# Splitting the store of one weight gradient: 128 rows from GpSimd become 5 and 55 rows from GpSimd and 68 from SyncE

## The chip, the cores and the metric

The kernel runs on one core of a Trainium2 chip. The metric is the device time of one execution in microseconds (us). Each engine of the core (TensorE or PE, VectorE or DVE, ScalarE or ACT, GpSimd or POOL, SyncE or SP) works through its own list of instructions and waits on semaphores for the others. Data moves between the device memory (DRAM) and the on-chip memory (SBUF, 128 partitions or rows) by 16 DMA engines; SyncE, ScalarE and GpSimd issue such transfers.

## The reference

The forward pass is a residual sum of a cached attention step and a gated MLP, for one token. The output is the forward value and all gradients for a given grad_out.

```python
x = A_x                                   # (1, 1, 640)
xn = _layernorm(x)
# attention: q = xn @ wq, 32 heads of 128; caches k, v are (1, 32, 8192, 128)
#   p = softmax(q k^T / sqrt(128));  o = p v;  A = o @ wo
# MLP: h = silu(xn @ w1) * (xn @ w3);  B = h @ w2
return x + A + B
...
_out, _vjp = jax.vjp(_f, A_x, A_k_cache, A_v_cache, A_wq, A_wo, B_w1, B_w3, B_w2)
_grads = _vjp(grad_out)
```

Each of the 32 heads has a K and a V cache of 8192 x 128 bf16 values, 2 MB each, and a gradient of the same size for both. The gradient of wo (4096 x 640), which the change is about, is an outer product: row (head, d) is o[head, d] times grad_out.

## The kernel before

The program works through the heads one after another. A head's K and V tiles are loaded into slots of the SBUF (10 slots of 128 x 8192 bf16), TensorE transposes and multiplies them (scores, probabilities, output, gradient of the probabilities), and then VectorE overwrites the same slots with the gradients of V and K (`outer`, line 464), which are stored from there. `store` (line 477) issues the 2 MB store and then calls `load_next` (line 122), which loads the next K or V tile into the oldest free slot; that load waits until the store from the slot has landed. All these transfers go through `fifo` (line 104), which issues them from SyncE in program order. The order on every engine is the one in which the program is written; nothing is rescheduled.

The projection weights wq and wo belong to 8 groups of 4 heads. `load_group` (line 109) loads one group's `wq_g` (128 x 5 x 512 bf16) and `wo_g` (128 x 4 x 640 bf16), 640 KB each. After the 4 heads of group g are done, during the next group's heads, the group is finished: in its first head `fin_od`, `fin_pe` and `fin_wo` (called at line 690, 714 and 702), and in the next two heads `fin_wq` in five pieces. `fin_wo` (line 512) overwrites the four 640-wide rows of `wo_g` by g_bc times o on VectorE (line 515) and stores the tile; the last piece of `fin_wq` stores `wq_g` and loads group g+3 into the same buffers (three sets of buffers).

The store itself is in `store_group` (line 505). For groups 0 to 6 it is one transfer of 128 rows from GpSimd (line 507). For group 7, the last, it is two transfers from SyncE: rows 0 to 59 and rows 60 to 127 (lines 509 and 510). In the DRAM a wo row of the tile is four pieces of 1,280 bytes, one for each head; in the SBUF it is one piece of 5,120 bytes.

The MLP is computed between heads 1 and 2 (line 551); its gradients leave from GpSimd. At the very end VectorE and ScalarE form the two small outputs (lines 836 to 862), which ScalarE stores.

`head` (line 740) sets the order around the change: with hh the head's number in its group, for hh = 0 the call of `fin_wo` (in `side_v`, line 782) comes after the K store of the head before and the load behind it (`outers_b`, line 776), and before the V store of the same head, which follows in the next call of `head`.

Of the kernel before, what the change touches and what calls it, by code (L numbers as in the profile page):

```python
# [16 lines left out]
P = 128  # L17
# [4 lines left out]
def kernel(  # L22
# [22 lines left out]
    nc = tc.nc  # L45
# [8 lines left out]
    GH = 4  # L54
# [26 lines left out]
    dwo_v = out_5.rearrange("(h p) c -> p h c", p=P)  # L81
# [22 lines left out]
    def fifo(out_, in_):  # L104
        nc.sync.dma_start(out_, in_)
# [396 lines left out]
        for hh in range(GH):  # L502
            out_row(G_["od_bf"][:, hh, 0:1], G_["wo"][:, hh, :])

    def store_group(g, dst, t):
        if g < NG - 1:
            nc.gpsimd.dma_start(dst, t[:])
            return
        for lo, hi in ((0, 60), (60, P)):
            fifo(dst[lo:hi], t[lo:hi])  # L510

    def fin_wo(g):
        G_ = grp[g]
        for hh in range(GH):
            nc.vector.tensor_scalar(G_["wo"][:, hh, :], g_bc[:], G_["od"][:, hh, 0:1], None, ALU.mult)
        store_group(g, dwo_v[:, g * GH:(g + 1) * GH, :], G_["wo"])

    def fin_wq(g, ci):
        G_ = grp[g]
        wq_g, dqb = G_["wq"], G_["dqb"]  # L520
        nc.vector.scalar_tensor_tensor(wq_g[:, ci, :], wq_g[:, ci, :], 1.0, dqb, ALU.mult, ALU.mult,  # L521
                                       accum_out=dxa[:, ci, g:g + 1])
        nc.vector.tensor_scalar(wq_g[:, ci, :], dqb, xn_col[:, ci:ci + 1], None, ALU.mult)
        if ci == NC - 1:
            store_group(g, dwq_v[:, :, g * GW:(g + 1) * GW], wq_g)
            grp.pop(g)
            if g + 3 < NG:
                load_group(g + 3, nc.gpsimd)
# [170 lines left out]
    def side_v(h):  # L699
        g, hh = divmod(h, GH)  # L700
        if hh == 0 and g > 0:
            fin_wo(g - 1)
        elif hh == 1 and g > 0:
            fin_wq(g - 1, 2)
        elif hh == 2 and g + 1 < NG:
            prep_new(g + 1)
            prep_do(g + 1, 0)
        elif hh == 3 and g + 1 < NG:
            prep_cm(g + 1, hd[h]["m"][:, 324:324 + 4 * GH])
# [120 lines left out]
    fin_od(NG - 1)  # L830
    fin_pe(NG - 1)
    fin_wo(NG - 1)
    for ci in range(NC):
        fin_wq(NG - 1, ci)
# [58 lines left out]
```

## Time and profile before

| | us |
|---|---|
| median of 3 timed runs | 730.84 |
| lowest and highest of them | 729.69, 731.25 |
| profiled execution: span, first to last instruction | 729.3 |
| DMA share of q1 (issued by SyncE and ScalarE) / q0 (issued by GpSimd) | 90.1% / 8.4% |
| data moved, read + written | 151.34 + 151.34 MB |
| mean rate over the span | 416 GB/s |

No other time of the profiled execution is given than its span. The median of the timed runs is 1.5 us above it; differences are worked out within the profile and then added to the median.

A profile page is read like this. "busy" is the time in which an engine executes; the waits say for whom an engine stood idle, and a wait for a DMA names the transfer that landed last. In rows over 40 slices a digit is the busy share in tenths. "DMA" is the mean busy share of the 16 DMA engines: a share of 0.25 is four engines busy. In tables by stretches the columns are the stretch, its length, the busy us of PE, the weight loads (PEld), DVE, ACT and POOL with their instruction counts, then the granted TensorE clock, the DMA share and the rate in GB/s. Entries with SPq are SyncE's transfers and waits. A transfer is cut into packets, each carried by one DMA engine, and each engine reports when its part is done; the trace holds a record of every packet and every such report.

### The profile page before, as it was taken

The page shows a single profiled execution, that of the slowest core. Times are in us where ns is not written, and L with a number is a line of the kernel's source. Part 1 is how long each engine was busy: PE and PEld are TensorE (multiplying, and loading weights), DVE is VectorE, ACT ScalarE, POOL GpSimd, SP SyncE. Part 2 cuts the span into 40 slices and gives each one's busy share as a digit, 9 for nine tenths or more (in the row PEclk, how much of TensorE's full clock was granted, in tenths as well). Part 3 has the DMA queues.
Part 4 walks back from the last instruction along what each step waited for, and adds up shares of the span by engine and source line. Part 5 has one row for each costly group of instructions (what it writes and reads, how often), then busy time and mean ns, then how long its engine had stood idle before and what let it go on. Part 6 is the DMA issues. An engine that isn't in the chain of part 4 may idle for free.

```text
span 729.3 us, 12905 instructions
## 1 busy us (share of the span) xinstructions
PE 600.8 (82%) x5186; PEld 375.4 (51%) x5193; DVE 461.3 (63%) x811; ACT 375.8 (52%) x727; POOL 28.2 (4%) x43
## 2 busy tenths in 40 slices
PE   4989589999999989887897798877897878977930
PEld 2556366665566556554454454544564545544520
DVE  4179646677868886676466755655746765667482
ACT  3740736665666566554465554554564555645510
POOL 0010100000100000001000000000000000000000
PEclk9996799999999999999999999998999999999965
DMA  8999999999999999999999999999999999999994
GB/s 353 404 411 422 427 427 428 417 426 426 414 417 426 430 426 426 428 428 428 422 428 430 428 425 428 427 428 429 424 429 425 430 429 430 428 427 430 430 396 161
DMA packets 28005, 303.53 MB, mean 416 GB/s; under 512 B 2804, under 2 KB 5304, under 8 KB 11304
## 3 DMA queue, kind: packets, MB, share of 16 engines
q1 hardware_dynamic: 22518, 277.70, 90.1%
q0 software_dynamic: 5408, 24.99, 8.4%
q8 instruction: 41, 0.67, 0.4%
q14 instruction: 20, 0.16, 0.1%
q10 hardware_dynamic: 18, 0.01, 0.0%
HBM read 151.34 MB, written 151.34 MB: 415 GB/s over the span
## 4 chain that ended last, share of the span: by engine, by line
DMA 55%; PE 34%; DVE 6%; ACT 2%; issue 1%; SPq 0%; ACTq 0%; DVEq 0%
DMA kv<-in_A_v_cache_dram 21%; DMA out_dram<-kv 18%; PE pT L318 16%; DMA kv<-in_A_k_cache_dram 14%; PE sA L339 5%; PE dA L339 3%; PE X L433 3%; DVE kv L466 3%; PE m L356 2%; DMA wo_g<-in_A_wo_dram 2%; PE gu_ps L556 1%; ACT KT L320 1%; PE dh_ps L567 1%; DVE wq_g L521 1%; PE acc L199 1%
## 5 line engine op out<-in xcount | busy, mean ns | idle before, releaser
L320 ACT COPY KT<-pT 128x512 f32<-128x512 f32 x512 | 287.9, 587 | 230.0 <-PE pT L318 210.3
L318 PE MATMUL pT<-ident_f,kv 128*128 128x128 f32 x2048 | 306.0, 288 | 62.5 <-DMA kv<-in_A_k_cache_dram 35.3
L318 PEld LDWEIGHTS pT<-ident_f,kv 128*128 128x128 f32 x2048 | 235.4, 148 | 155.1 <-PE pT L318 50.0
L466 DVE TENSOR_TENSOR kv<-qd,U 128x4096 bf16<-128x4096 bf16 x64 | 146.1, 2285 | 0.0
L466 DVE TENSOR_TENSOR kv<-qd,P 128x4096 bf16<-128x4096 bf16 x64 | 143.6, 2285 | 0.0
L433 PE MATMUL X<-kv,Z 128*32 128x512 bf16 x1024 | 95.2, 407 | 1.8 <-DVE Z L450 1.8
L339 PE MATMUL dA<-KT,qz 128*32 128x512 bf16 x512 | 83.5, 405 | 0.0
L339 PE MATMUL sA<-KT,qz 128*32 128x512 bf16 x512 | 83.5, 406 | 0.0
L416 DVE SCALAR_TENSOR_TENSOR U<-m,P 128x64 bf16<-128x64 f32 x32 | 7.5, 234 | 87.2 <-PE m L356 87.2
L382 DVE TENSOR_REDUCE mrow<-m 128x1 f32<-128x64 f32 x32 | 7.2, 224 | 69.6 <-PE m L356 69.5
L433 PEld LDWEIGHTS <-Z 128*32 128x32 bf16 x1024 | 33.0, 100 | 34.5 <-issue 7.1
L339 PEld LDWEIGHTS <-qz 128*32 128x32 bf16 x1024 | 29.6, 95 | 40.5 <-issue 38.0
L356 PE MATMUL m<-selc,KT 64*128 64x64 f32 x256 | 30.5, 242 | 7.9 <-ACT KT L346 7.8
L356 PEld LDWEIGHTS m<-selc,KT 64*128 64x128 f32 x256 | 21.5, 144 | 29.9 <-ACT KT L346 20.0
L376 ACT CAST qd<-pT 128x256 bf16<-128x256 f32 x32 | 11.9, 372 | 40.3 <-DVE kv L466 31.6
L389 DVE TENSOR_REDUCE negM<-m 128x1 f32<-128x128 f32 x32 | 9.3, 292 | 33.0 <-PE m L386 33.0
L521 DVE SCALAR_TENSOR_TENSOR wq_g<-wq_g,side 128x512 bf16<-128x512 bf16 x40 | 27.3, 683 | 0.0
L257 DVE SCALAR_TENSOR_TENSOR side<-wo_g,g_bc 128x640 bf16<-128x640 bf16 x32 | 26.2, 820 | 0.7 <-DMA wo_g<-in_A_wo_dram 0.3
L448 DVE SCALAR_TENSOR_TENSOR U<-m,P 128x128 bf16<-128x128 f32 x32 | 11.4, 355 | 16.4 <-PE m L446 16.4
L406 DVE RECIPROCAL rZ<-m 128x1 f32<-128x1 f32 x32 | 5.3, 167 | 24.1 <-PE m L400 24.1
L346 ACT COPY KT<-dA 64x512 f32<-64x512 f32 x32 | 18.6, 582 | 2.9 <-PE dA L339 2.9
L346 ACT COPY KT<-sA 64x512 f32<-64x512 f32 x32 | 18.5, 579 | 2.0 <-PE sA L339 1.7
(161 smaller groups left out, 372.2 us busy)
## 6 DMA issues: line engine op xcount, KB each, us to landing
out_dram<-kv SPq DMA_DIRECT2D x64, 2048.0 KB, 31.0
kv<-in_A_k_cache_dram SPq DMA_DIRECT2D x32, 2048.0 KB, 26.3
kv<-in_A_v_cache_dram SPq DMA_DIRECT2D x32, 2048.0 KB, 26.3
wq_g<-in_A_wq_dram POOLq DMA_DIRECT2D x7, 640.0 KB, 13.4
wo_g<-in_A_wo_dram POOLq DMA_DIRECT2D x7, 640.0 KB, 19.1
out_dram<-wo_g POOLq DMA_DIRECT2D x7, 640.0 KB, 11.9
out_dram<-wq_g POOLq DMA_DIRECT2D x7, 640.0 KB, 13.4
kv<-in_B_w_dram SPq DMA_DIRECT2D x2, 1728.0 KB, 29.2
```

What stands on the lines that cost most here:

```text
L257: nc.vector.scalar_tensor_tensor(junk[:], G_["wo"][:, hh, :], 1.0, g_bc[:], ALU.mult, ALU.mult, accum_out=G_["do"][:, hh:hh + 1])
L318: nc.tensor.transpose(pT[:, k * P:(k + 1) * P], W3[:, 4 * c + k, :], ident_f[:])
L320: nc.scalar.copy(KT[:].rearrange("p k w -> p (k w)"), pT[:])
L339: nc.tensor.matmul(S_[kind][q:q + QW, :], lhsT=S_["qz"][:, o:o + QW], rhs=KTb[c][:, par, :], start=(c0 == 0 and par == 0), stop=(c0 == NCH ...
L346: nc.scalar.copy(XS[0:QH].rearrange("p k w -> p (k w)"), S_.pop(kind)[0:QH, :])
L356: nc.tensor.matmul(S_["m"][:, b0:b0 + 4 * J].rearrange("p (x c k t) -> p k x c t", x=4, k=4, t=2)[:, k], lhsT=XS[0:QH, k, :], rhs=selc[0:Q ...
L376: nc.scalar.copy(qd[:].rearrange("p a d -> p (a d)"), hd[h].pop("ps_r"))
L389: nc.vector.tensor_reduce(S_["negM"][:], S_["m"][:, 2 * J:2 * J + P], AX.X, ALU.max, negate=True)
L433: nc.tensor.matmul(xg["X"][q:q + QW, :], lhsT=Z[:, o:o + QW], rhs=W[:, N4 * i:N4 * (i + 1)], start=(slot == 0 and i < 4), stop=(slot == NS ...
L448: nc.vector.scalar_tensor_tensor(S_["U2"][:], S_["V"][:, 0:J].unsqueeze(2).to_broadcast([P, J, 2]), S_["m"][:, OC + NS:OC + NS + 1], S_["P ...
L466: nc.vector.tensor_tensor(dst[:, lo * DH:hi * DH].rearrange("p (j a b) -> p j a b", a=DH // 2, b=2), vec.rearrange("p (a b) -> p a b", b=2 ...
L521: nc.vector.scalar_tensor_tensor(wq_g[:, ci, :], wq_g[:, ci, :], 1.0, dqb, ALU.mult, ALU.mult, accum_out=dxa[:, ci, g:g + 1])
```

## The change

The store of wo's gradient for groups 1 to 5 leaves as three transfers: rows 0 to 4 and rows 5 to 59 from GpSimd, and rows 60 to 127 from SyncE. Groups 0, 6 and 7 and all of wq's stores stay as they were. Values and bytes are the same.

```diff
-    def store_group(g, dst, t):
+    def store_group(g, dst, t, split=False):
+        if split:
+            for lo, hi in ((0, 5), (5, 60)):
+                nc.gpsimd.dma_start(dst[lo:hi], t[lo:hi])
+            fifo(dst[60:P], t[60:P])
+            return
         if g < NG - 1:
             nc.gpsimd.dma_start(dst, t[:])
             return
...
-        store_group(g, dwo_v[:, g * GH:(g + 1) * GH, :], G_["wo"])
+        store_group(g, dwo_v[:, g * GH:(g + 1) * GH, :], G_["wo"], 1 <= g <= 5)
```

In the instruction lists GpSimd gets five more transfers and SyncE five more; each of SyncE's stands between a load of a K or V tile and the store of the next gradient. The other engines' instructions and their order are the same.

## Prediction

> **What bounds the kernel now.** First I read the page: how busy the engines are and, beside it, what the DMA engines do.
>
> ```profile
> PE 600.8 (82%) x5186; PEld 375.4 (51%) x5193; DVE 461.3 (63%) x811; ACT 375.8 (52%) x727; POOL 28.2 (4%) x43
> DMA  8999999999999999999999999999999999999994
> GB/s 353 404 411 422 427 427 428 417 426 426 414 417 426 430 426 426 428 428 428 422 428 430 428 425 428 427 428 429 424 429 425 430 429 430 428 427 430 430 396 161
> q1 hardware_dynamic: 22518, 277.70, 90.1%
> q0 software_dynamic: 5408, 24.99, 8.4%
> ```
>
> No compute engine is full, but all 16 DMA engines are, from the first slice to the last but one. At 428 GB/s each moves 428/16 = 26.8 GB/s. q1 is what SyncE and ScalarE issue, q0 what GpSimd issues. Next, SyncE's waits:
>
> ```profile
> SPq L105 <- DMA out_dram<-kv: 490.1, 54, 15.1
> SPq L105 <- DVE kv L466: 87.0, 12, 13.4
> ```
>
> SyncE waits 490 us for stores to land before it may load into their buffers; for DVE it waits a fifth of that. So the time is the work of the DMA engines, and what counts is which of the 16 ends last. That is seen in the table by stretches, cut fine at the end (the last two columns are the DMA share and GB/s):
>
> ```profile
> 100.00:690.00 590.00, 516.73 (x4425) 319.59 (x4431) 380.29 (x623) 329.20 (x656) 19.59 (x24) 0.96 1.01 426
> ...
> 718.00:720.00 2.00, 0.00 (x0) 0.00 (x0) 0.00 (x0) 0.00 (x0) 0.00 (x0) 0.50 0.61 197
> 720.00:722.00 2.00, 0.00 (x0) 0.00 (x0) 0.00 (x0) 0.00 (x0) 0.00 (x0) 0.50 0.22 77
> 722.00:725.00 3.00, 0.00 (x0) 0.00 (x0) 0.00 (x0) 0.00 (x0) 0.00 (x0) 0.50 0.32 111
> 725.00:726.00 1.00, 0.00 (x0) 0.00 (x0) 0.00 (x0) 0.00 (x0) 0.00 (x0) 0.50 0.27 94
> 726.00:727.60 1.60, 0.00 (x0) 0.00 (x0) 0.00 (x0) 0.00 (x0) 0.00 (x0) 0.50 0.07 26
> ```
>
> Up to 690 the share is full (1.01). From 722 to 725 it is 0.32, which is five of 16 engines, and after 726 it is 0.07, one engine. The SyncE timeline says what they carry:
>
> ```profile
> 711.74 3.42 SPq L105 DMA_DIRECT2D out_dram<-wo_g  x2
> 715.27 5.96 SPq L105 DMA_DIRECT2D out_dram<-wq_g  x2
> ```
>
> The second issue of the last line, at 720.97, is the 68-row wq store of group 7. In the trace's packet records four engines carry it: 85 packets of 1,024 bytes each, 46 ns apart, from 721.8 to 725.7–726.2. The fifth busy engine is a straggler that is only then finishing its kv stores; it ends at 727.6, 1.7 us before the span does.
>
> The same records give each store's completion engine by engine. The 2 MB store issued at 673.87 was done on five engines by 688.7–689.4, on two at 693.6, on eight at 695.5–699.1, and on the straggler at 706.7. The five keep this lead from about 220 us on; the lag of the others grows slowly. Nobody idles before 690, so an engine that gets more bytes falls behind, and one that gets fewer catches up.
>
> **The change, part by part.** Five times (groups 1 to 5) one 640 KB store from GpSimd becomes three. The bytes stay; their spread over the 16 engines does not.
>
> *The 128-row store that goes.* 128/16 = 8 rows of 5,120 bytes for each engine. Such a packet on q0 takes 200 ns: 8 x 0.20 = 1.6 us off every engine, per group.
>
> *The 68-row store on SyncE.* The nearest row is the same shape in group 7: four engines, 17 rows each. Its 1,280-byte packets run 52 ns apart when undisturbed: 17 x 4 x 52 ns = 3.5 us. Beside other small packets at the end they took 4.0 to 4.5 us. I take 3.5, as the neighbours in mid-run are 16 KB packets, and keep 4.5 for the range.
>
> *The 5- and 55-row stores on GpSimd.* No row shows them. In this trace 60 rows ran on 15 engines, 68 on 4 and 128 on 16, so I expect 5 rows on five engines (one each) and 55 on eleven (five each). Which ones is open: each of the four loaded engines gets 1 row if the two transfers share out the 16, up to 6 if both take the same engines. I take 3, near the mean of 60/16 = 3.75: 0.6 us; ends 0.2 and 1.2.
>
> *Sum.* A loaded engine gains 3.5 + 0.6 - 1.6 = 2.5 us per group, 12.5 us over five (ends: 2.1 x 5 = 10.5 and 4.1 x 5 = 20.5). The others lose 2 to 7 rows per group, 0.4 to 1.4 us; with 5 rows left it is 0.6, 3 us over five. The straggler carried 20, not 105, of the wq packets at the end, so it isn't one of the four: it ends near 724.6.
>
> The Trainium skill ("DMA: Bandwidth & Descriptors", section "Why a DMA increments its semaphore by 16 and not by 1") says that a transfer runs on the largest number of engines up to 16 that divides its rows; 60, 68 and 128 here agree. It adds that on this path fewer than 16 are taken in turn, which no run here shows; by it 5 + 11 share out the 16, the four get 1 row, and the end would come 2 us earlier than I say. The same page's "Rules for kernel authors" speaks against the change: two transfers to disjoint partition ranges gain nothing, since both spread over all 16 engines. The trace differs in one point, as 68 rows did not spread (0.32 of the engines); by the rule as written the time would not move.
>
> *Where the four stand.* In mid-run every transfer runs on all 16 engines, so nothing there tells which four these are; I use the end. A small ScalarE store of one 640-byte packet found its engine idle at 714.5, and one of the four fetched instructions at 715.3 with nothing before it. Seven engines were idle then: the five leaders and the two behind them. I take the four for leaders. They finished the store issued at 684.79 by 694.2. Three kv stores remain, 8 packets of 16 KB at 0.608 us each: 3 x 4.87 = 14.6, so without starving they would be done at 708.8. With 12.5 us more: 721.3. Then group 7: 4 + 17 rows of wo (0.8 + 3.5) and 4 + 17 rows of wq (0.9 + 3.9) = 9.1: 730.4. The end was 727.6, so +2.8 us: a span of 732.1 for 729.3. The median of the runs shown, 730.84, lies 1.5 above that span; the forecast is 730.84 + 2.8 = **733.6 us**.
>
> What they had spare is used in this sum: 4.3 us without work near 696, and about 3 us waiting for the issues at 714.89 and 720.97. It is gone afterwards; late next are the four engines themselves, through the last 68-row store.
>
> *Issues and waits.* Five more issues on GpSimd (0.76 us each) and five on SyncE (0.27 to 0.45) lie in idle time: GpSimd is 4% busy and waits 35 us before such a store. Uncovered they would cost 5 x 1.2 = 6 us of issue time. The new SyncE store waits for DVE's wo_g rows; in program order it stands between a kv load and a kv store. DVE was done at 293.1 in group 2, and SyncE issued that load at 296.31 after a DMA wait, so it finds its data ready. The kv store behind it goes 0.4 us later; the leaders' queue still held 3.1 us when the load at 659.69 was issued. The completion counters of q1 are eight in turn; some kv stores now also wait for the eighth transfer before them. Four load-store pairs of 10.1 us are 40 us, and the slowest landing took 38.4: done, with 2 us to spare. GpSimd's next wo load now waits also for the SyncE part, which lands some 31 to 35 us after 296, before the wq store whose landing released that load's neighbour at 341.43. I count these at nothing.
>
> **The rivals.**
>
> *Faster: the straggler decides.* It sets 727.6 and loses 3 us (5 rows left) or 7 us (1 row left). If the four net under 1.5 us per group, 7.5 in all, their spare time swallows it and they end at 726 or a little earlier, since the last issues come after loads that no longer wait as long. For it: the straggler's 18 us lag. Against: 17 rows for 8 can't well net under 2.1. Price: 1.5 to 3 us less, about 728.5.
>
> *No change: balance.* With 1 row from GpSimd and 3.5 us per 68 rows the four end at 728.4, 0.8 us later: 731.6, the same within 0.2% (1.5 us, about what a measurement of this kernel can tell).
>
> *Much slower: the four are not leaders.* If they stand with the engines at 695.5–697.3, 7 us behind, they end 7 us later still: about 740.6. Against it speak the idle engines at 714.5 and 715.3; for it, that an engine which finished its kv stores at 714.9 could be the one that started the 68 rows at 715.72.
>
> *The change doesn't spread as said.* If 5 and 55 rows go to all 16 engines, each of the four gets 3.75 rows, 0.15 us more per group than I take, 0.8 in all: 734.4, inside the forecast. If the 68 rows too went to all 16, nothing would change: 730.8.
>
> **How the numbers follow.** Forecast, four leaders overloaded, 732.4 to 737: 0.45. Much slower, 737 to 742: 0.15. Balance: 0.2. Faster: 0.2. So faster 0.2, same 0.2, slower 0.6. The forecast's own range comes from 10.5 us (731.6) to about 16 us; the whole of 20.5 would be 741.6. The range goes from 728.5, the faster rival's price, to 741.
>
> **What would show it.** Right: the DMA share at 0.25 in the last 5 us or more (four engines, no straggler), the sixteen completions of a mid-run kv store with the four moved back by 2.5 us after each of groups 1 to 5, and SyncE's waits for out_dram<-kv still the largest. Wrong: a last stretch at 0.07 that ends earlier than 727.6 (the straggler's rival), or a share below 1 before 690, which would mean that queues ran dry. It would also be wrong if DVE or ACT appeared among the waits of the new store.

## The result and the profile after

The changed kernel takes 749.34 us (median of 4 runs, 746.75 to 752.08) against 730.96 us for the kernel before: a ratio of 1.0253, 95% interval 1.0234 to 1.0272. It is slower, as forecast, but by 18.4 us where 2.8 were forecast, and outside the range. The profiled execution's span grew from 729.3 to 746.6 us.

The rows over 40 slices of the page of the changed kernel; a slice is 18.7 us:

```profile
DMA  9999999999999999999999899999999999999993
GB/s 354 404 410 422 426 428 428 428 426 425 423 420 426 417 416 425 413 423 351 427 421 423 376 366 429 422 427 376 383 431 410 429 372 409 430 427 427 429 430 152
```

The rate now has four dents, at slices 19, 23 and 24, 28 and 29, and 33: 351 to 383 GB/s in place of some 428. They are 90 us apart, one for each of groups 2 to 5. In finer stretches, the first dent and the deepest part of the second (columns as before: the last two are DMA share and GB/s):

```profile
338.00:340.00 2.00, 2.00 (x17) 1.33 (x16) 2.00 (x2) 1.07 (x2) 0.00 (x0) 1.00 0.74 276
...
428.00:430.00 2.00, 2.00 (x16) 0.97 (x12) 2.00 (x2) 1.44 (x4) 0.00 (x0) 1.00 0.25 94
```

A quarter of the DMA engines is idle at 338 to 340, and at 428 to 430 only four of the 16 are busy. This is the sign that the prediction named for itself being wrong: queues ran dry before 690. SyncE's timeline says why (start, duration, transfer):

```profile
230.64 16.44 SPq L105 DMA_DIRECT2D out_dram<-kv  x1
...
317.48 0.34 SPq L105 DMA_DIRECT2D kv<-in_A_v_cache_dram  x1
317.91 0.29 SPq L105 DMA_DIRECT2D out_dram<-wo_g  x1
318.29 20.73 SPq L105 DMA_DIRECT2D out_dram<-kv  x1
339.11 1.84 SPq L105 DMA_DIRECT2D kv<-in_A_k_cache_dram  x1
...
407.34 22.18 SPq L105 DMA_DIRECT2D out_dram<-kv  x1
...
496.77 21.88 SPq L105 DMA_DIRECT2D out_dram<-kv  x1
...
585.88 21.20 SPq L105 DMA_DIRECT2D out_dram<-kv  x1
```

The new 68-row issue itself takes 0.29 us. The kv store behind it takes 20.73 us: SyncE stands inside this issue, and the next load goes out at 339.11. In the kernel before no issue of a kv store in this stretch takes over 0.95 us. I call this **the hold** from here on. SyncE's waits have changed in kind:

```profile
SPq L105 <- DMA out_dram<-kv: 375.9, 45, 15.1
SPq L105 <- DVE kv L466: 86.8, 16, 13.3
SPq L105 <- DVE Z L450: 74.7, 8, 18.6
```

490.1 us of waiting for kv stores have become 375.9, since the time is now spent inside issues: the five holds add up to 102.4 us. The last line (1.4 us in the kernel before) is mostly these holds again, put down to a VectorE instruction that ended during them, and a wait for VectorE would be a rival to what follows. It is not that: VectorE had written the gradient that a held store carries 3.7 to 19.1 us before the store's issue began (in group 3 at 389.9, the issue at 407.3).

The end has changed owner. The last stretches of the changed kernel:

```profile
742.00:745.00 3.00, 0.00 (x0) 0.00 (x0) 0.00 (x0) 0.00 (x0) 0.00 (x0) 0.50 0.10 34
745.00:746.60 1.60, 0.00 (x0) 0.00 (x0) 0.00 (x0) 0.00 (x0) 0.00 (x0) 0.50 0.02 6
```

One or two engines are busy. In the packet records the last of them finishes its kv packets at 736.6 and then carries 84 wo packets and 105 wq packets to 745.4, as many as the four that carry the 68 rows: it is now one of them. Before, it was another one, with 16 and 20 small packets.

From the packet records I add up, over the 16 engines, the time in which they were busy and idle (engine-us; a sixteenth of a difference is a difference of time). The idle time depends on how the packets are laid out on the engines and is good to about a tenth. The lines below the second are runs told further on.

| kernel | busy | idle 20 to 690 us | idle after 690 us | sum, over 16, against before | span against before |
|---|---|---|---|---|---|
| before | 11,548 | 8 | 161 | | |
| changed | 11,710 | 138 | 160 | +18.2 | +17.3 |
| e2, no hold, same four engines | 11,637 | 14 | 288 | +13.9 | +12.9 |
| e3, hold, even load | 11,686 | 46 | 98 | +7.0 | +5.3 |
| e4, no hold, GpSimd | 11,611 | 12 | 122 | +1.7 | +1.1 |
| e16, no hold, GpSimd, same four | 11,621 | 14 | 241 | +9.9 | +9.3 |

In the changed kernel 130 of the 292 engine-us are idle time in the dents. The rest is busy time: the 16 KB packets took 625 ns in the mean instead of 616, and some three quarters of that lie in the 20 us behind a dent, when all engines start again together (mean there 678 to 697 ns; kv packets over 700 ns in the whole run: 494 instead of 153).

### The profile page after: what moved, and what is told of

It reads as the page before. It is cut to its first block, busy times and chain, and to the rows that moved or that the text cites. A ratio compares the mean times of both kernels' runs of the same rounds, so it can differ in the third digit from the quotient of the medians.

```text
span 746.6 us, 12942 instructions
## 1 busy us (share of the span) xinstructions
PE 603.0 (81%) x5186; PEld 376.3 (50%) x5193; DVE 460.3 (62%) x811; ACT 375.5 (50%) x727; POOL 31.2 (4%) x48
## 4 chain that ended last, share of the span: by engine, by line
DMA 52%; PE 32%; DVE 6%; ACT 4%; SPq 2%; issue 1%; ACTq 0%; DVEq 0%
DMA out_dram<-kv 24%; DMA kv<-in_A_k_cache_dram 19%; PE pT L318 15%; DMA kv<-in_A_v_cache_dram 7%; PE sA L339 4%; PE dA L339 3%; PE X L433 3%; DVE kv L466 3%; PE m L356 2%; SPq L105 2%; DMA wo_g<-in_A_wo_dram 2%; ACT KT L320 1%; ACT kv L642 1%; PE gu_ps L561 1%; PE dh_ps L572 1%
## 5 line engine op out<-in xcount | busy, mean ns | idle before, releaser
L433 PE MATMUL X<-kv,Z 128*32 128x512 bf16 x1024 | 98.8, 418 | 1.8 <-DVE Z L450 1.8
L356 PEld LDWEIGHTS m<-selc,KT 64*128 64x128 f32 x256 | 22.2, 148 | 32.8 <-ACT KT L346 20.3
## 6 DMA issues: line engine op xcount, KB each, us to landing
wq_g<-in_A_wq_dram POOLq DMA_DIRECT2D x7, 640.0 KB, 13.9
```

The costliest lines, as they stand in the source:

```text
L356: nc.tensor.matmul(S_["m"][:, b0:b0 + 4 * J].rearrange("p (x c k t) -> p k x c t", x=4, k=4, t=2)[:, k], lhsT=XS[0:QH, k, :], rhs=selc[0:Q ...
L433: nc.tensor.matmul(xg["X"][q:q + QW, :], lhsT=Z[:, o:o + QW], rhs=W[:, N4 * i:N4 * (i + 1)], start=(slot == 0 and i < 4), stop=(slot == NS ...
```

## The experiments

All are edits of the changed kernel unless said otherwise. Ratios are against the kernel before on the same chip (median 730.5 to 731.4 us). Two theories stood against each other first: the hold (A), and the extra rows on four engines (B, the prediction's own term).

**e1: the 68 rows from ScalarE.**

```diff
-            fifo(dst[60:P], t[60:P])
+            nc.scalar.dma_start(dst[60:P], t[60:P])
```

> The changed kernel with the 68-row transfer issued from ScalarE; the two GpSimd transfers as in the changed kernel. Bytes, packets and engines that carry them are the same. Load theory (four engines carry too many rows, 3.9 us of small packets per group each): the time stays at that of the changed kernel, 747 to 751 us. Stall theory (68 packets per engine stop up SyncE's own queue, so that the kv store behind them is issued 16 to 22 us late and the DMA engines run dry): no SyncE issue lasts over 2 us, the DMA share stays at 1.0 until the tail, and only the overload is left: 733 to 741 us.

Measured: 762.2 us, 1.0414 (1.0397 to 1.0432), which fits neither. No issue of a kv store is held, but SyncE now waits, by its waits and its timeline:

```profile
SPq L105 <- DMA out_dram<-wo_g: 153.4, 5, 31.9
```

```profile
210.49 0.35 SPq L105 DMA_DIRECT2D out_dram<-kv  x1
240.28 0.33 SPq L105 DMA_DIRECT2D kv<-in_A_k_cache_dram  x1
```

Five waits of some 31 us for the ScalarE transfer, one per group. Transfers of SyncE and ScalarE use eight completion counters in turn; a kv load of SyncE came to share one with the wo transfer (counter 102 for both in the first of these groups) and had to wait until that had landed, at 240.2. And that lands late: on ScalarE's queue its 68 packets per engine last from 225.6 to 239.9, 0.21 us each in the mean instead of 0.055. Until 235 each of the four engines sends one of them per 0.61 us, the time of one 16 KB packet of SyncE's queue: the two queues take turns. (ScalarE's transfers stand in the page as q10, 1,398 packets here and 18 in the kernel before; so q1, which the tables and lines ahead put down to SyncE and ScalarE, is SyncE's alone.) This run is a new wait of its own, and says nothing on A or B.

**e2: the 68 rows in four pieces.** One head at a time, 17 packets on each of the four engines, each piece behind another pair of kv store and load.

```diff
     def store(kind, h):
...
         load_next()
+        if pieces:
+            fifo(*pieces.pop(0))
...
-            fifo(dst[60:P], t[60:P])
+            for k in range(GH):
+                pieces.append((dst[60:P, k, :], t[60:P, k, :]))
+            fifo(*pieces.pop(0))
```

> The 68-row transfer stays on SyncE but is cut by head into four transfers of 68 x 640, issued one after each of four consecutive kv store and load pairs instead of all at once. The same four engines move the same bytes through the same queue. Load theory: 747 to 751 us. Stall theory: 17 packets per engine at a time fit, so no long issue: 733 to 741 us, as with ScalarE.

Measured: 740.94 us, 1.0135 (1.0113 to 1.0158). The longest issue of a kv store before 660 is 4.2 us, the dents are gone (14 engine-us idle before 690), and the time is 8.4 us below the changed kernel's. The other 9.5 us over the kernel before on the same chip (731.41; in the result it was 730.96, so the two don't add up to 18.4) stay, with the same bytes on the same four engines. Its last stretch shows one engine left:

```profile
737.00:741.00 4.00, 0.00 (x0) 0.00 (x0) 0.00 (x0) 0.00 (x0) 0.00 (x0) 0.50 0.08 29
```

**e3: hold with even load.** All 128 rows from SyncE as two halves of the columns, 64 packets of 640 bytes on each of 16 engines.

```diff
-            for lo, hi in ((0, 5), (5, 60)):
-                nc.gpsimd.dma_start(dst[lo:hi], t[lo:hi])
-            fifo(dst[60:P], t[60:P])
+            for c in (0, D // 2):
+                fifo(dst[:, :, c:c + D // 2], t[:, :, c:c + D // 2])
```

> All 128 rows from SyncE as two transfers back to back, the left and the right half of the 640 columns, nothing from GpSimd for these groups. Every engine gets 8 rows, as before the change, but 64 packets of 640 bytes at once instead of 68 of 1,280 on four engines. Load theory: the load is even again, 730 to 734 us. Stall theory: the kv store behind is held as in the changed kernel, now by all sixteen rings, the engines run dry after each of the five groups, 738 to 752 us.

Measured: 736.5 us, 1.0067 (1.0052 to 1.0082). The holds are as long as in the changed kernel:

```profile
318.03 21.73 SPq L105 DMA_DIRECT2D out_dram<-kv  x1
407.57 19.67 SPq L105 DMA_DIRECT2D out_dram<-kv  x1
```

So a hold of 20 us in itself costs about 1 us per group. The engines live on what was queued before, and only one larger dent is left (30 engine-us, near 338).

**e4: all three parts from GpSimd.**

```diff
-            fifo(dst[60:P], t[60:P])
+            nc.gpsimd.dma_start(dst[60:P], t[60:P])
```

> All three parts (5, 55 and 68 rows) from GpSimd, nothing added to SyncE. Load theory, if GpSimd too puts 68 rows on four engines: 745 to 751 us. Stall theory: SyncE is not held; 733 to 741 us if the 68 rows go to four engines, 730 to 733 us if GpSimd spreads them over all.

Measured: 732.65 us, 1.0017 (1.0006 to 1.0028). SyncE is as before:

```profile
SPq L105 <- DMA out_dram<-kv: 486.2, 54, 16.8
```

This left two readings open: either the overload of four engines is harmless and e2's pieces cost something of their own, or GpSimd's 68 rows did not fall on the same four engines each time. e16 decides.

**e5 and e6: how many packets make a hold.** e5 sends three heads at once (51 packets on four engines) and the fourth behind the next pair, by the lines that e2 has in `store`; e6 sends all 128 rows from SyncE in one transfer, the bytes of e3 in half as many packets (32 per engine).

```diff
-            fifo(dst[60:P], t[60:P])
+            fifo(dst[60:P, 0:3], t[60:P, 0:3])
+            pieces.append((dst[60:P, 3, :], t[60:P, 3, :]))
```

> The 68 rows leave SyncE as three heads at once (51 packets of 1,280 bytes on each of four engines) and the fourth head (17 packets) behind the next pair of kv store and load. Theory 'full queue' (an engine's queue has room for a limited number of packets, and SyncE's next issue is held until the slowest of the four has sent enough of the 16 KB packets that stand ahead): each packet fewer in the burst frees the store one 16 KB packet earlier, so the hold of 16 to 22 us falls by 17 x 0.61 = 10.4 us, to 6 to 12 us; less or no time in which engines run dry (138 us x engines before the cut, under 40 now); time 733 to 741. Rival 'price of the transfer' (a transfer of the wo gradient from SyncE holds what is behind it for a fixed time, whatever its packets): the hold stays at 16 to 22 us and the time at 747 to 752.

```diff
-            for lo, hi in ((0, 5), (5, 60)):
-                nc.gpsimd.dma_start(dst[lo:hi], t[lo:hi])
-            fifo(dst[60:P], t[60:P])
+            fifo(dst, t[:])
```

> All 128 rows leave SyncE in one transfer, nothing from GpSimd: 32 packets of 1,280 bytes on each of 16 engines, the same bytes as the two halves of 64 packets of 640 bytes, half the packets. Theory 'full queue': the hold falls by 32 x 0.61 = 20 us against the halves' 17 to 22 us, so to 0 to 2 us, and with even load the time is 730 to 734. Rival 'bytes' (what counts is the bytes that stand in the queue, the same here): the hold stays at 17 to 22 us and the time at 735 to 738.

Measured: e5 743.23 us, 1.0163 (1.0143 to 1.0183); e6 731.96 us, 1.0019 (1.0009 to 1.0030). Holds of e5, then the longest of e6:

```profile
231.01 8.91 SPq L105 DMA_DIRECT2D out_dram<-kv  x1
...
318.28 9.75 SPq L105 DMA_DIRECT2D out_dram<-kv  x1
...
492.50 11.65 SPq L105 DMA_DIRECT2D out_dram<-kv  x1
```

```profile
327.06 3.29 SPq L105 DMA_DIRECT2D out_dram<-kv  x1
```

The five holds of e5 are 7.5, 11.0, 11.7, 10.2 and 7.7 us shorter than those of the changed kernel, 9.6 in the mean, where 17 packets fewer were to give 10.4: 0.57 us for each, about the time of one 16 KB packet. With e3's bytes in half the packets the hold is all but gone. So packets per engine decide, not bytes. This is what a queue with a limited number of places per engine would do; the queue itself is in no record. The hold of e5 is only divided: the load and the fourth piece that follow are held in turn, as in group 2,

```profile
328.78 11.38 SPq L105 DMA_DIRECT2D out_dram<-wo_g  x1
```

and store, load and piece together take 16.2 to 21.9 us per group, as long as the hold of the changed kernel (16.4 to 22.2). But the store is out some 10 us earlier, and the engines have it to work on. e5's time missed its range: its dents are small (35 engine-us idle), and as in e2 some 9 us remain that A does not explain.

How long a hold lasts follows from the four engines' landings, as a transfer on four engines reports four. In the changed kernel and in e7 (below) each hold ends 7.0 to 8.2 us before the last of the four lands its part of the 68 rows (at 339.0 and 347.2 in group 2), 8.5 to 11.1 us in e12 and e13. Less 3.9 us for its 68 packets, that engine has then, in the changed kernel and e7, some 3 to 4 us of 16 KB packets left. So a hold lasts until the slowest of the four is nearly through with what stood ahead; engines that have less ahead of them run dry first, 12 of them at 428 to 430.

**e7, e12 and e13: splits in some groups only.**

```diff
-        store_group(g, dwo_v[:, g * GH:(g + 1) * GH, :], G_["wo"], 1 <= g <= 5)
+        store_group(g, dwo_v[:, g * GH:(g + 1) * GH, :], G_["wo"], g == 5)
```

(`g in (4, 5)` in e12, `g in (1, 5)` in e13.)

> Only group 5 is split as in the changed kernel; groups 1 to 4 leave in one 128-row transfer from GpSimd as in the kernel before. One hold of about 20 us, near 580. In the changed kernel the five holds moved the stream of kv packets by 0, 4.5, 6.3, 6.2 and 3.9 us. Theory 'each by itself' (a hold late in the kernel lets engines run dry whatever came earlier): 3 to 6 us later, 734 to 737. Rival 'lead used up' (the first hold costs nothing because the four engines still have their lead of some 18 us, as in group 1, and only later holds find it gone): 730 to 732.

> Groups 4 and 5 are split as in the changed kernel, groups 1 to 3 leave as before. Theory 'lead used up' (the first split in a row is free, the next finds the four engines some 2.5 us worse off): group 4 as group 1 (a hold of 11 to 16 us, no cost), group 5 as group 2 (hold about 20 us, kv stream 4.5 us later): 733.5 to 737. Rival 'one more is still free' (the four's lead is some 18 us, two splits take 5 of it): 730 to 732.

> Groups 1 and 5 are split as in the changed kernel. Groups 4 and 5 split gave holds of 11.3 and 15.5 us and 736.6 us, group 5 alone a hold of 11.0 us and 730.3 us. Theory 'the lead comes back' (the four engines gain again in the 350 us between): group 5's hold is 10 to 13 us, and the time 730 to 732. Rival 'the lead stays used up': group 5's hold is 14 to 18 us, and the time 734 to 738.

Measured: e7 730.28 us, 0.9996 (0.9985 to 1.0008); e12 736.62 us, 1.0084 (1.0068 to 1.0101); e13 735.89 us, 1.0071 (1.0057 to 1.0084). The hold of e7, the two of e12 and the two of e13:

```profile
575.95 11.01 SPq L105 DMA_DIRECT2D out_dram<-kv  x1
```

```profile
490.52 11.29 SPq L105 DMA_DIRECT2D out_dram<-kv  x1
575.94 15.49 SPq L105 DMA_DIRECT2D out_dram<-kv  x1
```

```profile
231.60 15.98 SPq L105 DMA_DIRECT2D out_dram<-kv  x1
...
575.20 16.71 SPq L105 DMA_DIRECT2D out_dram<-kv  x1
```

One split is free, though its store is held for 11 us. A second one costs 5 to 6 us, and it does not matter whether it comes 90 or 340 us after the first. What the four engines lose in one split they do not win back. The hold in group 5 shows the same from another side: 11.0 us when it is the only split, 15.5 and 16.7 when one went before. So do the landings of group 5's 68 rows: 589.9, 590.7, 594.8 and 594.9 in e7, 593.9, 595.7, 601.5 and 602.5 in e12, 593.9, 595.0, 601.3 and 602.3 in e13. The four are 4 to 8 us later after one earlier split, though the kv load ahead begins to land within 1.5 us of e7's: as it must be if both splits fall on the same four engines.

The packet records give the same picture in time. How much later than before the n-th of the 16,384 packets of 16 KB ended (us):

```
packet  before  changed    e3    e2    e4    e7   e12   e13
  5000   247.5     -1.5  -2.2  +0.5  +1.1  +0.1  -0.1  -0.5
  7000   330.6     +0.1  -1.4  +1.1  +2.3  +0.1  -0.1  +0.9
  8000   373.8     +4.4  +4.6  +0.1  +2.2  +0.1  -0.2  +0.8
 10000   456.9     +9.8  +6.9  +0.4  +2.7  +0.1  -0.2  +0.9
 12000   539.9    +14.1  +8.3  +0.6  +3.0  +0.0  +0.8  +0.9
 14000   619.6    +18.1  +9.2  +3.0  +3.6  +0.9  +3.5  +3.6
 16000   700.6    +16.9  +8.6  +5.9  +2.5  -0.3  +2.2  +2.4
  last   725.9    +10.7  +4.4  +6.0  +0.7  -1.4  -1.8  -2.0
```

Group 1 costs the changed kernel nothing (+0.1 at packet 7000); groups 2 to 5 cost it about 4.5 us each. In e12 and e13 the last kv packet ends earlier than before and yet the kernel ends 5 to 6 us later. Their loss must lie in the end piece: the stretches of e12 end with a few engines again.

```profile
726.00:730.00 4.00, 0.00 (x0) 0.00 (x0) 0.00 (x0) 0.00 (x0) 0.00 (x0) 0.50 0.24 83
730.00:733.00 3.00, 0.00 (x0) 0.00 (x0) 0.00 (x0) 0.00 (x0) 0.00 (x0) 0.50 0.09 33
```

**e9, e10, e11 and e14: an even end piece.** Group 7 as 64 and 64 rows (16 engines each), in the changed kernel (e9), in e2 (e10), in the kernel before (e11, the control) and in e12 (e14).

```diff
-        for lo, hi in ((0, 60), (60, P)):
+        for lo, hi in ((0, 64), (64, P)):
```

> The changed kernel, but group 7's wo and wq gradients leave SyncE as 64 and 64 rows (16 engines, 32 and 40 packets on each) instead of 60 and 68 (84 and 105 packets on the four). Theory 'the last engine is now one of the four': its small packets at the end fall by 52 x 52 ns and 65 x 42 ns, 2.7 + 2.7 = 5.4 us, so 742.5 to 745.5. Rival 'the kv stream alone sets the end' (the last engine is still another one, with 16 and 20 packets): it gets 16 and 20 packets more, 1.7 us, so 750 to 752.

> The four pieces of 17 packets, one behind each pair (740.9 us before), with group 7 as 64 and 64 rows. Theory 'end piece' (nothing is held in the five groups; the four have lost their lead to the extra rows, so the 68-row parts of group 7, 84 and 105 packets on them, set the end): up to 5 us less, 734 to 738. Rival 'pieces cost by themselves' (17-packet bursts in SyncE's queue slow the kv stream): 741 to 743.

> The kernel before with group 7 as 64 and 64 rows; the control of the two above. Theory 'another engine ends last in the kernel before' (16 and 20 small packets): it gets 16 x 52 ns and 20 x 42 ns more, 1.7 us: 732 to 733. Rival 'the four end it there too': 5 us less work on them, 726 to 730.

> Groups 4 and 5 split, group 7 as 64 and 64 rows. Theory 'end piece': in the pair's profile the last kv packet ended at 724.2, before the 725.9 of the kernel before, and one of the four ended last, at 732.8, after 84 and 105 small packets; with 32 and 40 on every engine it ends at about 724.2 + 3.3 = 727.5, 5 us earlier: 730 to 733. Rival 'the holds themselves cost it': 736 to 738.5.

| | with 60 and 68 rows | with 64 and 64 rows | ratio of the latter (95%) |
|---|---|---|---|
| kernel before | 730.6 | 732.90 | 1.0031 (1.0016 to 1.0045) |
| changed | 749.34 | 745.44 | 1.0200 (1.0181 to 1.0219) |
| e2 | 740.94 | 737.82 | 1.0099 (1.0084 to 1.0114) |
| e12 | 736.62 | 731.92 | 1.0015 (1.0004 to 1.0027) |

All four fell in the first theory's range. The even end is 2.3 us worse for the kernel before, where the last engine is not one of the four, and 3 to 5 us better wherever the four were given more rows in two groups or all five. So the last engine has become one of the four.

**e8: two even halves.** Rows 0 to 63 from GpSimd, 64 to 127 from SyncE: 16 packets per engine.

```diff
-            for lo, hi in ((0, 5), (5, 60)):
-                nc.gpsimd.dma_start(dst[lo:hi], t[lo:hi])
-            fifo(dst[60:P], t[60:P])
+            nc.gpsimd.dma_start(dst[0:64], t[0:64])
+            fifo(dst[64:P], t[64:P])
```

> Rows 0 to 63 leave from GpSimd and rows 64 to 127 from SyncE, both spread over 16 engines: 16 packets of 1,280 bytes on each engine in SyncE's queue. Theory 'full queue': 53 packets fewer than in the changed kernel on the fullest engine, so no hold (no kv store's issue over 3 us), even load, 730 to 732. Rival 'price of the transfer': hold of 16 to 22 us in each of the five groups and, the load being even, about what the two even halves gave, 735 to 738.

Measured: 731.6 us, 1.0016 (1.0006 to 1.0025); no issue over 1.7 us. Without hold and overload nothing is lost, and nothing gained.

**e15: one split with a lighter end piece**, an attempt to beat the kernel before: e7, and group 7 as 60, 63 and 5 rows.

```diff
-        for lo, hi in ((0, 60), (60, P)):
+        for lo, hi in ((0, 60), (60, 123), (123, P)):
```

> Group 5 alone split, and group 7 as 60, 63 and 5 rows (15, 9 and 5 engines; at most 48 and 60 small packets on an engine in place of 84 and 105). In the profile of group 5 alone one of the four ended last, at 727.2, the engine with the last kv packet at 726.9 at the latest. Theory 'the four end it': the end falls to that of the last kv packet, 724.5 + 16 x 52 ns + 20 x 42 ns = 726.2: 1 us less, 728.5 to 730. Rival 'issues': two more issues on SyncE, each some 2 to 4 us at the end, make the last transfer later: 731 to 734.

Measured: 732.97 us, 1.0030 (1.0018 to 1.0042). The time fell in the rival's range, but the landings show another cause. The 63 rows land on nine engines and the 5 on five, and the engine with the last kv packet (its last kv store lands at 725.5) is among both: it lands the six pieces of group 7 last, at 726.3, 727.7, 727.9, 728.7, 730.2 and 730.4. It carries 48 and 60 small packets in place of 16 and 20, 48 x 52 ns + 60 x 42 ns = 5.0 us behind its last kv packet at 725.0. What the four save, this engine takes. No kernel of this study beats the one before.

**e16: the overload fixed on four engines, from GpSimd.**

```diff
-            for lo, hi in ((0, 5), (5, 60)):
-                nc.gpsimd.dma_start(dst[lo:hi], t[lo:hi])
-            fifo(dst[60:P], t[60:P])
+            for lo, hi in ((60, P), (48, 60), (0, 48)):
+                nc.gpsimd.dma_start(dst[lo:hi], t[lo:hi])
```

> All 128 rows leave from GpSimd, as 68, 12 and 48 rows in this order. If a GpSimd transfer takes the next engines in turn (the Trainium skill, 'DMA: Bandwidth & Descriptors', section 'Why a DMA increments its semaphore by 16 and not by 1'), 68 rows take 4, 12 rows the other 12, 48 rows all 16: the turn comes back to its place and the same four engines carry 17 + 3 rows in each of the five groups, the others 1 + 3. Without the page: the four that carry 68 rows get about 12 rows of 0.2 us more than the 8 of before, 2.4 us per group, 12 us over five if they are the same each time. Theory 'a moving overload is harmless, a fixed one is not' (5, 55 and 68 rows from GpSimd moved from group to group): 736 to 742, like the 740.9 of the pieces on SyncE. Rival 'GpSimd's queue hides the overload' (its packets take turns with the 16 KB ones): 731 to 733.5, like the 732.7 of 5, 55 and 68 rows.

Measured: 739.85 us, 1.0121 (1.0101 to 1.0141), and no issue of SyncE over 2 us before 660. The end is two engines:

```profile
734.00:737.00 3.00, 0.00 (x0) 0.00 (x0) 0.00 (x0) 0.00 (x0) 0.00 (x0) 0.50 0.13 46
```

The same 68 rows from the same engine cost 1.2 us when the group's transfers are 5, 55 and 68 rows and 9.4 us when they are 68, 12 and 48, each against the kernel before on its chip. So e2's remaining 9.5 us need no price of pieces on SyncE: the overload is enough, as soon as it always falls on the same four. In e2 the landings show that it does. With 0.9 us taken off for the 17 packets of a group's first piece, the four stand 0 to 3 us behind the first engine's landing of the kv load ahead of it in group 1 (pieces at 250.6 to 253.5, the load's first landing at 249.8) and 8.5 to 18 us behind in group 5 (598.0, 601.2, 601.4 and 607.6; 588.5), where the slowest of the four is also the last of all 16. That the overload moved in e4 is inferred from the times, as no record names the engines. By the Trainium skill's "DMA: Bandwidth & Descriptors" ("Why a DMA increments its semaphore by 16 and not by 1") GpSimd's transfers on fewer than 16 engines go to the next engines in turn, while SyncE's always take the lowest-numbered; e2, e4 and e16 agree with it.

## Why the prediction was wrong

Its sign and its resource were right: the 16 DMA engines bound the kernel, the straggler was not one of the four (e11), and the four got later. The size failed in two steps.

*"I count these at nothing"* (issues and waits) failed first: 8.4 us (changed against e2). The prediction priced the new issue (0.27 to 0.45 us, and 0.29 was measured) and let the kv store behind it go "0.4 us later". It went 16 to 22 us later, because SyncE was held while the 68 packets stood ahead of it on each of four engines. A row of the kernel before could have warned. At its start SyncE issues `wq_g` and `wo_g` of group 0, 40 and 32 small packets on each engine, and the kv load behind them takes 3.23 us to issue instead of 0.3 to 0.5:

```profile
2.25 3.23 SPq L105 DMA_DIRECT2D kv<-in_A_v_cache_dram  x1
```

Only one kv load stood ahead there, and the hold was short. By e3 the hold alone is worth about 5 us; with the four engines late it is worth 8, since the other twelve run dry while they wait for them.

*"I take the four for leaders"* failed second: the overload alone made 9.4 to 9.5 us (e16, e2), not 2.8. The term of 2.5 us per group was about right: the bursts took 3.7 (e2) to 3.9 us per group in the mean where 3.5 was taken, and in e2 the four fell back by 2 to 4 us per group behind the first engine, which carries fewer rows than before. The rows that GpSimd's 5 and 55 put on them (3 taken) are in no record by engine. The place was wrong. In e7, up to group 5 the same program as before, the four landed their 68 rows at 589.9, 590.7, 594.8 and 594.9, and the kv load ahead landed from 586.4 on: less 3.8 us, two of the four were leaders and two stood 5 us behind, with that much less to spare. Reckoned afterwards, five us on top of the forecast's 733.6 is 738.6, near e16's 739.9. The rival "much slower: the four are not leaders" had the mechanism and 740.6. The engines idle at 714.5 and 715.3 that were held against it could not decide: leaders had already run dry near 696, so those behind had caught up. In the kernel before all four land group 7's 68 wo rows at 720.0 to 720.8, so no lead is left to read there.

*The others.* The straggler did lose work: its last kv packet ended 1.4 us earlier with one split and 1.8 to 2.0 with two, but by then the four ended later. The share of 0.25 at the end did not come; a single late engine of the four came instead (0.10 and 0.02). The wait for a shared completion counter was judged rightly for the changed kernel, where none is named, and came with 31 us in e1. That "the four get 1 row" by the skill's rule of turns does not follow from it: it holds if the turn starts at the first of the four, and where it stands no run shows. That GpSimd's next wo load finds its buffer free was wrong:

```profile
342.31 0.89 POOL L111 DMA_DIRECT2D wq_g<-in_A_wq_dram  x1 [11.77 <-DMA out_dram<-wq_g]
347.80 0.77 POOL L113 DMA_DIRECT2D wo_g<-in_A_wo_dram  x1 [4.61 <-PE m L386]
```

It goes 5.5 us later, behind the 68 rows' last landing at 347.2 (the row names TensorE, but the issue comes 0.6 us after that landing). It serves a group two groups later; what it costs was not tried by itself.

The rule that speaks against the change ("Rules for kernel authors", which the Trainium skill's "DMA: Bandwidth & Descriptors" states for two disjoint halves of the partitions) is borne out by e8, 1.0016 with 64 and 64 rows, whose halves run on all 16 engines. Neither that rule nor the row of 0.32 said that the change could lose.

What stays open: what exactly is full during the hold, and how many places it has; why many 16 KB packets take 1.1 us and more after a dent; and why the kv stream in e2 ends 6.0 us later but in e16 only 2.4, though both end the kernel some 9 us later. On the first, the Trainium skill's "DMA: Bandwidth & Descriptors" ("Queues, rings and completion order") gives each pair of queue and engine a ring of its own, which fits; no run here shows its length.

## What to carry to other kernels

Before a transfer is added to the queue that feeds the bound resource, count its packets on the fullest engine, not its bytes or its issue time: here 16 went through, 32 held the next store for 3.3 us at most, 51 held it for 9 to 14 us, and 68 for 11 to 22 us, until the slowest of the four engines was nearly through its backlog. A transfer on few engines hit the same engines every time from SyncE, so its cost added up over the whole kernel and showed at the end; rows in a multiple of 16 (e8) avoid that, and so did GpSimd's queue with 5, 55 and 68 rows (e4), but not with 68, 12 and 48 (e16). And where such engines stand is to be read from the landings of a transfer that runs on them alone, one number per engine, rather than from an idle engine at the end.

## What was not expected of the hardware

- An issue on SyncE took 11 to 22 us when 64 or 68 small packets per engine were put into its queue ahead of it; 51 gave 9 to 14, 32 at most 3.3, 16 at most 1.7.
- 68 packets of 1,280 bytes took 3.7 us on an engine in SyncE's queue and some 14 us in ScalarE's, where they alternate with SyncE's 16 KB packets.
- After a dent, in which a quarter to three quarters of the engines ran dry, the 16 KB packets took 0.68 to 0.70 us in the mean for the next 20 us instead of 0.61, and one in twenty 1.1 us or more.
- The same 68 rows from GpSimd cost 1.2 or 9.4 us, according to the row counts of the transfers sent beside them.
